# A reordered opening in a fused attention and feed-forward kernel: first values loaded before the last two head pairs, single transposes, four gate steps ahead of the first Silu

## The chip, the cores and the metric

The kernel runs on one core of one Trainium2 chip. The metric is the device time of one execution in microseconds (us), lower is better. Each kernel was run several times. The kernel before took 344.77 us as the median of three runs when the prediction was made.

## The reference

Inputs are `q`, `k`, `v` of shape 8 x 8 x 576 x 64 (batch, heads, sequence, head size) and three weight matrices. It is causal attention with a window of 64, and then a SwiGLU feed-forward over the 4608 tokens.

```python
def _attn_ref(q, k, v):
    scores = scale * np.matmul(q, k.transpose(0, 1, 3, 2))   # scale = 1/8
    rel = pos[:, None] - pos[None, :]
    scores = np.where((rel >= 0) & (rel < 64), scores, -1000000000.0)
    attn = np.exp(scores - np.max(scores, axis=-1, keepdims=True))
    attn = attn / (np.sum(attn, axis=-1, keepdims=True) + 1e-09)
    return np.matmul(attn, v)

def _moe_ref(x, w_gate, w_val, w_out):          # x: 4608 x 512, the heads side by side
    g = x @ w_gate                              # 512 x 1536
    silu = g * (1.0 / (1.0 + np.exp(-g)))
    return silu * (x @ w_val) @ w_out           # 1536 x 512
```

## The kernel before

The 4608 tokens are nine tasks of 512. One task needs scores, exps, sums and values for four pairs of heads, then twelve "gate steps" (each makes one 128-row block of the hidden layer: four matmuls with gate weights, four with value weights), then four projections with their output stores.

Tasks 0 and 1 are the opening. The sync queue loads their q and k as float32, a compute engine casts them to bf16, and the TensorE transposes them. All later tasks are loaded by the GpSimd queue, which casts on the way, and are turned by the VectorE. The first task's values are loaded as float32, cast by GpSimd and copied ("shifted") by the VectorE. Load order and GpSimd's order in the opening:

```python
    for u in range(4):
        load_pair(0, u)                    # q and k of one head pair, 256 KB each
    load_pair(1, 0)
    load_pair(1, 1)
    load_v(nc.sync, staged[0, "v"], 0, (0, 1))
    load_pair(1, 2)
    load_v(nc.sync, staged[0, "v"], 0, (2, 3))
    load_pair(1, 3)
    # ... later, GpSimd (and some VectorE, ScalarE) casts, in this order:
    for u in range(4):
        cast_pair(0, u)
    cast_pair(1, 0)
    cast_pair(1, 1)
    cast_v(0, (0, 1))
    cast_pair(1, 2)
    weights_gv(0, 128)                     # first block of gate and value weights
    cast_v(0, (2, 3))
    cast_pair(1, 3)
    weights_gv(128, 384)                   # second block
    weights_gv(384, 768)                   # third block
    weights_gv(768, 1152)
    load_v(nc.gpsimd, v1[1], 1)
    weights_gv(1152, 1536)
```

GpSimd both casts and issues the weight loads, in program order, so a late cast delays all the weights behind it. The TensorE's side of the opening, with `warm` matmuls that only keep it busy:

```python
    turn_pe(0)
    for i in range(1, 6):
        turn_pe(i)                         # transposes of q and k of pair i
        score(i - 1)
        if i > 2 and i % 2:
            sum_pair(i - 3)
        if i > 3:
            keep_warm(2)
    # ... score(5), turn_pe(6), score(6), sum_pair(4), turn_pe(7), score(7), keep_warm between
    for u in range(4):
        values_of(0, u)
    begun.append(gate_value(0, 0))         # three gate steps before the first Silu
    sum_pair(6)
    begun.append(gate_value(0, 1))
    begun.append(gate_value(0, 2, ps_a.tile([P, 2, 512], FP32, name="gv_ps", tag="a")))
    load_qk(2)                             # GpSimd: q, then k of task 2
    for c in range(2):
        weights_o(6 * c, 6 * c + 6)
    set_silu()                             # the ScalarE's table load: from Exp to Silu
    for m in range(12):
        (begun[m] if m < 3 else gate_value(0, m))()
        # ... task 1's values between them
    for m in range(12):
        gate_value(1, m)()
        if m % 3 == 1:
            turn(2, m // 3)                # VectorE: needs task 2's q and k
```

A gate step ends with a Silu on the ScalarE and a product on the VectorE. A projection's result goes through one of two SBUF buffers to the store:

```python
        def finish():
            nc.scalar.activation(sg[:], g_ps, AF.Silu)
            nc.vector.tensor_mul(hT[t][:, m, :], sg[:], v_ps)
    # in project():
        os_ = fsb.tile([P, 512], FP32, name="os_", tag="os_", bufs=2)
        nc.vector.tensor_copy(os_[:], o_ps[:])
        # ... store os_ with one or four DMAs
```

The softmax here doesn't subtract the row's maximum and nothing guards it: scores larger than these inputs give would overflow.

## Time and profile before

| | before |
|---|---|
| time, median of the runs of this comparison | 344.95 us (four runs, 344.46 to 345.17) |
| span of the profiled run | 342.5 us |
| TensorE busy | 326.3 us, 95% |
| first gate matmul | 25.92 us |
| wait of the fourth gate step | 0.54 us, for the first Silu |
| first transpose of task 2's k | 55.41 us, no wait |
| wait for an output buffer | 1.33 us on the TensorE at 134.51 us |

The page of the kernel before: the span, the busy time of each engine, busy tenths in 40 slices (8.6 us each), and, from the groups of instructions, the gate matmuls with their idle time ahead of them and what ended most of it.

```profile
span 342.5 us, 7084 instructions
PE 326.3 (95%) x2779; PEld 155.6 (45%) x2824; DVE 209.4 (61%) x309; ACT 162.2 (47%) x226; POOL 142.7 (42%) x253
...
PE   7869999999999998999999999999999999999994
...
PEclk9999999999999999999999999999999999999998
...
L286 PE MATMUL g_ps<-xT,wg 128*128 128x512 bf16 x416 | 108.6, 379 | 2.5 <-DVE os__1921 L306 1.3
```

PE is the TensorE. It is idle for 16 us of 342, and the first slices hold most of that.

The timeline of the kernel before (start, duration, engine, line, operation; in brackets the idle time before it and what ended it). SP is the sync engine, POOL is GpSimd, DVE the VectorE, ACT the ScalarE. Here and below single lines are picked from a view; what stands between them is left out.

```profile
17.27 0.90 POOL L157 DMA_DIRECT2D wg<-in_moe_w_gate_dram  x1
20.58 0.69 POOL L393 CAST qk_b<-k_f 128x512 bf16<-128x512 f32 x1
21.22 0.74 POOL L157 DMA_DIRECT2D wg<-in_moe_w_gate_dram  x1
25.92 1.07 PE L286 MATMUL g_ps<-xT,wg 128*128 128x512 bf16 x3 [0.16 <-issue]
32.51 1.02 PE L286 MATMUL g_ps<-xT,wg 128*128 128x512 bf16 x4 [0.54 <-ACT sg L293]
...
34.23 1.03 PE L286 MATMUL g_ps<-xT,wg 128*128 128x512 bf16 x4
...
55.41 1.28 DVE L197 STREAM_TRANSPOSE kT<-k_s 128x512 bf16<-128x512 bf16 x1
58.23 1.03 PE L286 MATMUL v_ps<-xT,wv 128*128 128x512 bf16 x4
...
133.77 0.69 DVE L306 COPY os__1921<-o_ps 128x512 f32<-128x512 f32 x1 [2.56 <-DMA out_dram<-os__1786]
134.51 1.02 PE L286 MATMUL g_ps<-xT,wg 128*128 128x512 bf16 x4 [1.33 <-DVE os__1921 L306]
```

The second weight block is issued at 21.22, straight after the last pair's cast, so the opening's weights hang on those casts. The k transpose at 55.41 starts without a wait, but task 2's k lands, by the packet records, at 55.22: 0.19 us of room.

### The profile page before, as it was taken

The page shows a single profiled execution, that of the slowest core. Times are in us where ns is not written, and L with a number is a line of the kernel's source. Part 1 is how long each engine was busy: PE and PEld are TensorE (multiplying, and loading weights), DVE is VectorE, ACT ScalarE, POOL GpSimd, SP SyncE. Part 2 cuts the span into 40 slices and gives each one's busy share as a digit, 9 for nine tenths or more (in the row PEclk, how much of TensorE's full clock was granted, in tenths as well). Part 3 has the DMA queues.
Part 4 walks back from the last instruction along what each step waited for, and adds up shares of the span by engine and source line. Part 5 has one row for each costly group of instructions (what it writes and reads, how often), then busy time and mean ns, then how long its engine had stood idle before and what let it go on. Part 6 is the DMA issues. An engine that isn't in the chain of part 4 may idle for free.

```text
span 342.5 us, 7084 instructions
## 1 busy us (share of the span) xinstructions
PE 326.3 (95%) x2779; PEld 155.6 (45%) x2824; DVE 209.4 (61%) x309; ACT 162.2 (47%) x226; POOL 142.7 (42%) x253
## 2 busy tenths in 40 slices
PE   7869999999999998999999999999999999999994
PEld 4533444444444453444444544454445444454441
DVE  5663657764456773786478657775777476754431
ACT  3866223353343565347633763376337733673310
POOL 4796469234456995426520989066200000000000
PEclk9999999999999999999999999999999999999998
DMA  7999999998899939919970799879500330020013
GB/s 260 298 140 190 185 166 134 169 227 147 203 202 239 118 61 213 233 30 169 182 178 1 116 184 175 54 123 214 138 2 24 78 78 0 14 82 31 1 34 93
DMA packets 83362, 44.43 MB, mean 130 GB/s; under 512 B 64640, under 2 KB 77952, under 8 KB 83328
## 3 DMA queue, kind: packets, MB, share of 16 engines
q0 software_dynamic: 46656, 21.28, 51.2%
q1 hardware_dynamic: 35744, 21.64, 22.6%
q10 hardware_dynamic: 928, 1.05, 1.1%
q8 instruction: 22, 0.36, 0.4%
q14 instruction: 12, 0.10, 0.1%
HBM read 53.02 MB, written 9.44 MB: 182 GB/s over the span
## 4 chain that ended last, share of the span: by engine, by line
PE 86%; DMA 6%; DVE 2%; POOL 2%; issue 1%; ACT 1%; SPq 1%; DVEq 0%
PE v_ps L286 26%; PE o_ps L301 26%; PE g_ps L286 26%; PE s_ps L219 3%; PE ao_ps L264 2%; PE d_ps L248 2%; DMA v_f<-in_v_dram 2%; DMA out_dram<-os__1786 2%; DMA k_f<-in_k_dram 2%; POOL qk_b L393 1%; DVE xT L270 1%; SPq L318 1%; POOL v L146 1%; SPq L73 0%; ACT L324 0%
## 5 line engine op out<-in xcount | busy, mean ns | idle before, releaser
L293 ACT ACTIVATE sg<-g_ps 128x512 f32<-128x512 f32 x107 | 63.8, 597 | 118.3 <-PE g_ps L286 84.9
L294 DVE TENSOR_TENSOR hT<-sg,v_ps 128x512 bf16<-128x512 f32 x107 | 74.1, 693 | 65.3 <-PE v_ps L286 58.2
L286 PE MATMUL g_ps<-xT,wg 128*128 128x512 bf16 x416 | 108.6, 379 | 2.5 <-DVE os__1921 L306 1.3
L286 PE MATMUL v_ps<-xT,wv 128*128 128x512 bf16 x420 | 108.9, 379 | 0.5
L301 PE MATMUL o_ps<-wo,hT 128*128 128x512 bf16 x407 | 96.8, 380 | 1.4 <-issue 0.3
L107 POOL DMA_DIRECT2D k_s<-in_k_dram x112 | 60.7, 551 | 31.7 <-DMA q_s<-in_q_dram 21.1
L286 PEld LDWEIGHTS <-wg 128*128 128x128 bf16 x432 | 41.8, 98 | 52.4 <-issue 2.8
L286 PEld LDWEIGHTS <-wv 128*128 128x128 bf16 x432 | 42.2, 98 | 51.3 <-issue 0.4
L301 PEld LDWEIGHTS <-hT 128*128 128x128 bf16 x432 | 39.7, 98 | 45.1
L234 ACT ACTIVATE E<-s_ps 128x1024 bf16<-128x1024 f32 x36 | 35.4, 1020 | 14.5 <-PE s_ps L219 9.5
L270 DVE TENSOR_TENSOR xT<-ao_ps,r 128x512 bf16<-128x512 f32 x36 | 24.7, 690 | 19.3 <-ACT r L254 18.1
L197 DVE STREAM_TRANSPOSE kT<-k_s 128x512 bf16<-128x512 bf16 x28 | 35.9, 1283 | 0.0
L253 ACT ACTIVATE r<-d_ps 128x512 f32<-128x512 f32 (+1 forms) x32 | 20.6, 643 | 27.6 <-PE d_ps L248 27.6
L146 POOL CAST v<-v_f 128x512 bf16<-128x512 f32 x24 | 15.4, 652 | 31.4 <-DMA v_f<-in_v_dram 30.1
L236 DVE TENSOR_TENSOR E<-E,mask 128x1024 bf16<-128x1024 bf16 x24 | 17.2, 718 | 10.4 <-ACT E L234 10.3
L87 POOL DMA_DIRECT2D q_s<-in_q_dram x24 | 13.1, 553 | 23.4 <-DVE qT L190 13.8
L254 ACT ACTIVATE r<-r 128x512 f32<-128x512 f32 (+1 forms) x32 | 21.8, 683 | 1.0
L190 DVE STREAM_TRANSPOSE qT<-q_s 128x512 bf16<-128x512 bf16 x28 | 19.7, 704 | 0.0
L264 PEld LDWEIGHTS <-v 128*64 128x64 bf16 x576 | 13.6, 112 | 6.3 <-issue 2.5
L264 PE MATMUL ao_ps<-E,v 128*64 128x64 bf16 x576 | 15.1, 196 | 1.2 <-DVE xT L270 0.8
L248 PE MATMUL d_ps<-E,ones 128*64 128x512 bf16 x72 | 13.6, 393 | 0.9 <-ACT E L234 0.7
L219 PE MATMUL s_ps<-qT,kT 64*64 64x128 bf16 (+1 forms) x640 | 12.9, 211 | 0.8 <-DVE kT L180 0.8
(89 smaller groups left out, 177.5 us busy)
## 6 DMA issues: line engine op xcount, KB each, us to landing
k_s<-in_k_dram POOLq DMA_DIRECT2D x112, 56.0 KB, 4.6
v_f<-in_v_dram SPq DMA_DIRECT2D x24, 256.0 KB
q_s<-in_q_dram POOLq DMA_DIRECT2D x24, 248.0 KB, 6.7
q_f<-in_q_dram SPq DMA_DIRECT2D x8, 256.0 KB
v<-in_v_dram POOLq DMA_DIRECT2D x16, 128.0 KB, 7.7
k_f<-in_k_dram SPq DMA_DIRECT2D x6, 256.0 KB
wo<-in_moe_w_out_dram POOLq DMA_DIRECT2D x2, 768.0 KB, 10.0
v<-v SPq DMA_DIRECT2D x6, 256.0 KB
```

The lines of the kernel that those rows point to most:

```text
L107: nc.gpsimd.dma_start(k_s[p0:p0 + 32, g, :, 0:w], k[b, a:H:2, s:s + P].rearrange("u (r e) d -> r u (e d)", e=4) [:, :, 32 * c:32 * c + w],)
L197: nc.vector.transpose(dst[:, u, :].rearrange("r (g x e) -> r g e x", g=4, e=4), k_s[:, :, u].rearrange("r g (e d) -> r g e d", d=D)[:, :, ...
L219: nc.tensor.matmul(blocks(s_ps[64 * c:64 * c + 64, h], t, lo, hi), zero[r] if src is None else src[r, u, x:x + 64], blocks(qT[r], t, lo, h ...
L234: nc.scalar.activation(E[:], s_ps[:], AF.Exp, scale=0.125)
L253: nc.scalar.activation(x, d_ps[:], AF.Ln)
L254: nc.scalar.activation(x, x, AF.Exp, scale=-1.0)
L264: nc.tensor.matmul(blocks(o_ps[64 * h:64 * h + 64], t, m, m + 1), (v1, v2)[m // 4][t % 2][:, m % 4, 2 * u + h, :] if t == LAST else (v2, v ...
L270: nc.vector.tensor_mul(xT[t][:, u, :], o_ps[:], inverse.pop((t, u)))
L286: nc.tensor.matmul(ps, w[:, c, P * m:P * m + P], xT[t][:, c, :], start=(c == 0), stop=(c == 3),)
L293: nc.scalar.activation(sg[:], g_ps, AF.Silu)
L294: nc.vector.tensor_mul(hT[t][:, m, :], sg[:], v_ps)
L301: nc.tensor.matmul(o_ps[:], hT[t][:, c, P * s:P * s + P], wo[:, c, :], start=(c == 0), stop=(c == 11),)
```

## The change

It should bring the TensorE to its gate steps earlier. The first task's values are loaded and used ahead of the last two head pairs of task 1; q and k get transposes and PSUM buffers of their own; loads and casts are single and stand where they are used; sums stand where their exps end; four gate steps, not three, precede the first Silu, so that the ScalarE's table load is hidden behind more matmuls. The last two weight blocks are also cut into three, task 1's values are loaded after column 1024 of the weights and not after 1152, and the opening has ten warm matmuls, not eight. The diff, cut to its core:

```diff
-    def transposes(t, u):
-        tp = ps_f.tile([P, 2, 512], BF16, name="tp", tag="g")
+    def transposes(t, u, i):
+        tp = ps_f.tile([P, 512], BF16, name="tp", tag="gv"[i])
 # ... one of q and k per call, each copied by the VectorE as before
-    for u in range(4):
-        load_pair(0, u)
-    load_pair(1, 0)
-    load_pair(1, 1)
-    load_v(nc.sync, staged[0, "v"], 0, (0, 1))
-    load_pair(1, 2)
-    load_v(nc.sync, staged[0, "v"], 0, (2, 3))
-    load_pair(1, 3)
+    for i in range(6):
+        load_heads(i // 4, i % 4)
+    load_v(nc.sync, staged[0, "v"], 0)
+    load_heads(1, 2)
+    load_heads(1, 3)
 # ... the block of casts and weights_gv (above) goes; in its place:
+    cast_heads(0, 0, nc.scalar.copy, on_v)
     turn_pe(0)
     for i in range(1, 6):
+        cast_heads(i // 4, i % 4, nc.scalar.copy if i == 1 else on_p, on_p)
         turn_pe(i)
 # ...
-        if i > 3:
+        if i > 2:
             keep_warm(2)
-    shift_v(0, nc.vector.tensor_copy, 0, 2)
     score(5)
     keep_warm(2)
+    for i in range(0, 4, 2):
+        cast_v(0, (i, i + 1))
+        shift_v(0, on_v, i, i + 2)
+    keep_warm(2)
+    weights_gv(0, 128)
+    values_of(0, 0)
+    values_of(0, 1)
+    cast_heads(1, 2, on_p, on_p)
     turn_pe(6)
+    sum_pair(4)
+    values_of(0, 2)
     score(6)
-    sum_pair(4)
-    keep_warm(2)
-    shift_v(0, nc.vector.tensor_copy, 2, 4)
+    cast_heads(1, 3, on_p, on_p)
     turn_pe(7)
+    values_of(0, 3)
+    weights_gv(128, 384)
+    weights_gv(384, 768)
+    weights_gv(768, 1024)
+    load_v(nc.gpsimd, v1[1], 1)
+    weights_gv(1024, 1280)
+    weights_gv(1280, 1536)
     score(7)
-    for u in range(4):
-        values_of(0, u)
     begun.append(gate_value(0, 0))
 # ...
+    begun.append(gate_value(0, 3, wide()))
 # ...
-        (begun[m] if m < 3 else gate_value(0, m))()
+        (begun[m] if m < 4 else gate_value(0, m))()
```

More of the change, by code (lines that the diff above doesn't have):

```diff
@@ L165, in weights_o @@
         )
-    def transposes(t, u):
-        tp = ps_f.tile([P, 2, 512], BF16, name="tp", tag="g")
-        if u == 0:
-            queries[t] = att.tile([P, 4, 512], BF16, name="qT", tag="qT")
-        for i in range(2):
-            for e in range(4):
-                for h in range(2):
-                    nc.tensor.transpose(
-                        tp[64 * h:64 * h + 64, i, P * e:P * e + P],
-                        staged[t][:, i, 2 * u + h, e, :], identb[:],
-                    )
-        nc.vector.tensor_copy(queries[t][:, u, :], tp[:, 0, :])
-        nc.vector.tensor_copy(
-            kT[t % 2][:, u, :].rearrange("p (r e) -> p r e", e=4),
-            tp[:, 1, :].rearrange("p (e r) -> p r e", e=4),
-        )
+    def transposes(t, u, i):
+        tp = ps_f.tile([P, 512], BF16, name="tp", tag="gv"[i])
+        for e in range(4):
+            for h in range(2):
+                nc.tensor.transpose(
+                    tp[64 * h:64 * h + 64, P * e:P * e + P],
+                    staged[t][:, i, 2 * u + h, e, :], identb[:],
+                )
+        if i == 0:
+            nc.vector.tensor_copy(queries[t][:, u, :], tp[:])
+        else:
+            nc.vector.tensor_copy(
+                kT[t % 2][:, u, :].rearrange("p (r e) -> p r e", e=4),
+                tp[:].rearrange("p (e r) -> p r e", e=4),
+            )
     def turn(t, u):
@@ L330, with load_heads @@
     new_v(0)
-    def load_pair(t, u):
+    def load_heads(t, u):
         hs = slice(2 * u, 2 * u + 2)
@@ L385, with cast_heads @@
         staged[t] = cast.tile([P, 2, H, 4, D], BF16, name="qk_b", tag=f"c{t}")
-    def cast_pair(t, u):
+        queries[t] = att.tile([P, 4, 512], BF16, name="qT", tag="qT")
+    def cast_heads(t, u, *copies):
         hs = slice(2 * u, 2 * u + 2)
-        for i in range(2):
-            copy = nc.gpsimd.tensor_copy
-            if t == 0 and u < 2 - i:
-                copy = nc.vector.tensor_copy if i else nc.scalar.copy
+        for i, copy in enumerate(copies):
             copy(staged[t][:, i, hs], raw[t][i][:, hs])
-    for u in range(4):
-        cast_pair(0, u)
-    cast_pair(1, 0)
-    cast_pair(1, 1)
-    cast_v(0, (0, 1))
-    cast_pair(1, 2)
-    weights_gv(0, 128)
-    cast_v(0, (2, 3))
-    cast_pair(1, 3)
-    weights_gv(128, 384)
-    weights_gv(384, 768)
-    weights_gv(768, 1152)
-    load_v(nc.gpsimd, v1[1], 1)
-    weights_gv(1152, 1536)
+    on_v, on_p = nc.vector.tensor_copy, nc.gpsimd.tensor_copy
     def values_of(t, u):
@@ L419, in score, with turn_pe @@
         scores(i // 4, i % 4)
-    def turn_pe(i):
-        transposes(i // 4, i % 4)
+    def turn_pe(i, *which):
+        for x in which or range(2):
+            transposes(i // 4, i % 4, x)
     def sum_pair(i):
@@ L426, in sum_pair, with wide @@
         sums(t, (u, u + 1), ps_a.tile([P, 2, 512], FP32, name="d_ps", tag="a"))
+    def wide():
+        return ps_a.tile([P, 2, 512], FP32, name="gv_ps", tag="a")
+    cast_heads(0, 0, nc.scalar.copy, on_v)
     turn_pe(0)
     for i in range(1, 6):
+        cast_heads(i // 4, i % 4, nc.scalar.copy if i == 1 else on_p, on_p)
         turn_pe(i)
@@ L433 @@
             sum_pair(i - 3)
-        if i > 3:
+        if i > 2:
             keep_warm(2)
-    shift_v(0, nc.vector.tensor_copy, 0, 2)
     score(5)
     keep_warm(2)
+    for i in range(0, 4, 2):
[6 more added lines that the diff above has]
+    cast_heads(1, 2, on_p, on_p)
     turn_pe(6)
+    sum_pair(4)
+    values_of(0, 2)
     score(6)
-    sum_pair(4)
-    keep_warm(2)
-    shift_v(0, nc.vector.tensor_copy, 2, 4)
+    cast_heads(1, 3, on_p, on_p)
     turn_pe(7)
+    values_of(0, 3)
[5 more added lines that the diff above has]
+    weights_gv(1280, 1536)
     score(7)
-    for u in range(4):
-        values_of(0, u)
     begun.append(gate_value(0, 0))
@@ L450 @@
     begun.append(gate_value(0, 1))
-    begun.append(gate_value(0, 2, ps_a.tile([P, 2, 512], FP32, name="gv_ps", tag="a")))
+    begun.append(gate_value(0, 2, wide()))
+    begun.append(gate_value(0, 3, wide()))
     load_qk(2)
```

## The prediction

> **What bounds it now.** The TensorE is 95% busy (busy shares); from 32.5 us on the timeline shows gate, value and projection matmuls almost back to back (one gate step: 1.73 us). Only the opening has holes: the first gate matmul starts at 25.92, and the fourth gate step at 32.51, after a 0.54 us wait for the first Silu.
>
> Behind the opening stands the DMA. By the packet records, the last sync-queue loads (task 1, pair 3) land at 19.8 and about 20.3, and GpSimd casts them at 20.02 and 20.58 (timeline). The first gate/value weights are issued at 17.27, the second block at 21.22, right after those casts. From about 24 us the GpSimd queue streams without a break: second block landed 25.2/27.0, third 29.5/31.4, fourth 33.4/35.3, task 1's values 36.2 to 38.7, last weights 40.6/42.6, task 2's q 43.8 to 47.8, its k 48.2 to 55.22. The VectorE's first transpose of that k starts at 55.41: only 0.2 us of room.
>
> **What the change does.** The value products (four of 0.37 us, serialised by 0.69 us evictions from 23.42 to 25.9) move ahead of and between the last two head pairs, transposes get a buffer per half, one sums group moves forward, and four gate steps instead of three precede the first Silu.
>
> The Trainium skill ("DMA: Bandwidth & Descriptors", Queues, rings and completion order) says that each DMA engine round-robins between queues and consumes each ring in order (the loads' semaphores here do complete in issue order); putting values ahead of pairs moves no total: the last pair should still land near 20. GpSimd does four value casts (0.61 each), two weight issues (0.8 each), four pair casts: the second weight block is issued at 21.2 to 21.7, no earlier than now; the weight stream is 0 to 0.3 late.
>
> **Estimate.** The last q/k casts end near 21.4, and then the VectorE does copies (0.42, 0.68) and evictions (0.69) in order: first gate matmul near 24.5 to 25. The sums' Ln and Exp, table load and Silu follow; the fourth step no longer waits for the Silu but for its value weights (31.4 to 31.7). The fifth step, 34.23 now, starts near 32.4: TensorE about 1.8 us ahead. The first turn then wants k at 53.6, but it lands at 55.2 to 55.5. The VectorE works in order, so the next hT product ends no earlier than now (57.2), and the value matmul of task 1's step 4 (58.23 now) gains only 1.0 less the stream's lateness. Gain 0.8 us.
>
> **Predicted time 344.0 us, 342.7 to 344.9 (8 in 10).** Faster by over 2%: 0.01; within 2%: 0.98; slower: 0.01.
>
> **What would show it.** First gate matmul at 24 to 25.3. Second weight block issued at 21 to 21.8 and landed at 25 to 27.5. Fourth gate step waiting for weights, not for the Silu. In the waits, a new one of the VectorE's k transpose for the k DMA, 1 to 2 us, near 54, and a TensorE hole of 0.5 to 1.2 us near 57. After 60 us the same schedule, shifted by under 1.2 us.
>
> **What would make it wrong.** If the earlier values let GpSimd issue the second weight block clearly before 20.5, the stream and task 2's k move up and up to 2 us are gained. If port conflicts between VectorE copies and GpSimd slow the casts ("SBUF — State Buffer", Who interferes with whom; here a cast took 0.90 instead of 0.61 us at 15.68 beside a VectorE copy), the stream is later and the gain vanishes.

## The result, and the profile after

The kernel after took 343.58 us as the median of four runs (342.99 to 343.94) beside 344.95 us before. The ratio is 0.996, with a 95% interval of 0.994 to 0.998, so it is the same by the 2% rule. Here and below a ratio is the mean time of one kernel's runs over that of the other's runs of the same rounds, so not quite the ratio of the medians.

The page of the kernel after, the same parts, and from the groups the k transposes:

```profile
span 342.2 us, 7134 instructions
PE 329.9 (96%) x2826; PEld 156.2 (46%) x2826; DVE 209.1 (61%) x309; ACT 162.2 (47%) x226; POOL 143.6 (42%) x255
...
PE   7969999999999999999999999999999999999994
...
PEclk9989999999999999999999999999999999999999
...
L196 DVE STREAM_TRANSPOSE kT<-k_s 128x512 bf16<-128x512 bf16 x28 | 36.0, 1284 | 1.6 <-DMA k_s<-in_k_dram 1.6
```

Two things are new: the third slice has a lower clock, and the k transposes, which waited for nothing before, wait 1.6 us for the k DMA. The TensorE's busy time is 3.6 us higher in a span 0.3 us shorter. That is hardly more work done (two more warm matmuls): part of it is matmuls at half clock, and some matmul records can be missing from a trace (before lists 2779 matmuls beside 2824 weight loads, after 2826 beside 2826).

The timeline of the kernel after, for the same places:

```profile
19.50 0.61 POOL L388 CAST qk_b<-q_f 128x512 bf16<-128x512 f32 x1 [0.89 <-DMA q_f<-in_q_dram]
20.17 0.41 PE L172 MATMUL tp<-identb,qk_b 128*64 128x128 bf16 x8 [2.00 <-POOL qk_b L388]
22.00 0.74 POOL L157 DMA_DIRECT2D wg<-in_moe_w_gate_dram  x1
25.53 1.04 PE L285 MATMUL g_ps<-xT,wg 128*128 128x512 bf16 x4
...
32.85 1.04 PE L285 MATMUL gv_ps<-xT,wv 128*128 128x512 bf16 x4 [0.45 <-DMA wv<-in_moe_w_val_dram]
33.73 1.03 PE L285 MATMUL g_ps<-xT,wg 128*128 128x512 bf16 x4
...
56.60 1.32 DVE L196 STREAM_TRANSPOSE kT<-k_s 128x512 bf16<-128x512 bf16 x1 [1.62 <-DMA k_s<-in_k_dram]
58.49 1.02 PE L285 MATMUL v_ps<-xT,wv 128*128 128x512 bf16 x4 [0.61 <-DVE hT L293]
...
133.44 0.69 DVE L305 COPY os__1932<-o_ps 128x512 f32<-128x512 f32 x1 [1.96 <-DMA out_dram<-os__1797]
134.18 1.02 PE L285 MATMUL g_ps<-xT,wg 128*128 128x512 bf16 x4 [0.73 <-DVE os__1932 L305]
```

Line by line against before: the first gate matmul is only 0.39 us earlier (25.92 to 25.53). The fifth step is 0.50 us earlier (34.23 to 33.73). The first k transpose is 1.19 us **later** (55.41 to 56.60), because k lands later (56.32 by the packet records, 55.22 before). The matmul behind it is 0.26 us later (58.23 to 58.49). So at 58 us the changed kernel is behind. At 134 us it is ahead again by 0.33 us, since the wait for the output buffer is 0.73 and not 1.33 us. That 0.33 us then stays to the end (spans 342.5 and 342.2).

### The half-clock stretch

The windows view gives busy times in stretches that I cut at the clock's own steps, which come every 3.41 us (3413 ns). Columns: stretch, its length, busy time (and instructions) of PE, PEld, DVE, ACT and POOL, granted clock, mean busy share of the DMA engines, GB/s. The kernel before:

```profile
15.99:19.40 3.41, 2.32 (x62) 1.34 (x50) 1.87 (x4) 2.59 (x3) 3.41 (x5) 1.00 0.85 223
19.40:22.81 3.41, 2.17 (x28) 0.97 (x24) 2.96 (x4) 2.99 (x3) 3.41 (x7) 1.00 0.81 78
```

The kernel after:

```profile
18.31:21.72 3.41, 1.32 (x36) 0.96 (x36) 1.90 (x4) 0.08 (x2) 2.42 (x5) 1.00 0.95 136
21.72:25.13 3.41, 3.24 (x80) 2.49 (x78) 2.37 (x5) 2.97 (x3) 3.41 (x6) 0.50 0.55 68
```

Before, the TensorE is 2.32 and 2.17 us busy in the two stretches (68% and 63%), and the clock stays at 1.00. After, the 2.00 us wait ahead of the transposes at 20.17 leaves only 1.32 us busy (39%), and the next stretch runs at 0.50. The Trainium skill ("TensorE: Matmul & The Clock Gate", What's actually happening) says that the clock is judged in a free-running window of 3413 ns and has two states, half and full; the step lengths here agree. It names as the rule "no PE-idle gaps >~3.4µs" (HAM oscillation); here a hole of 2.00 us was enough. The same load was late in most traces of the changed opening (see e1), and what the half clock cost is sorted out under e9 to e11.

### The profile page after: what moved, and what is told of

It reads as the page before. It is cut to its first block, busy times and chain, and to the rows that moved or that the text cites. A ratio compares the mean times of both kernels' runs of the same rounds, so it can differ in the third digit from the quotient of the medians.

```text
span 342.2 us, 7134 instructions
## 1 busy us (share of the span) xinstructions
PE 329.9 (96%) x2826; PEld 156.2 (46%) x2826; DVE 209.1 (61%) x309; ACT 162.2 (47%) x226; POOL 143.6 (42%) x255
## 4 chain that ended last, share of the span: by engine, by line
PE 83%; DMA 8%; SPq 3%; DVE 1%; POOL 1%; ACT 1%; issue 1%; DVEq 0%
PE g_ps L285 26%; PE v_ps L285 26%; PE o_ps L300 25%; DMA wv<-in_moe_w_val_dram 3%; PE ao_ps L263 2%; PE s_ps L218 2%; PE d_ps L247 2%; DMA out_dram<-os__1797 2%; DMA q_f<-in_q_dram 2%; SPq L126 2%; DMA k_f<-in_k_dram 1%; SPq L317 1%; POOL qk_b L388 1%; ACT E L233 1%; DMA out_dram<-os__1734 0%
## 5 line engine op out<-in xcount | busy, mean ns | idle before, releaser
L300 PE MATMUL o_ps<-wo,hT 128*128 128x512 bf16 x432 | 99.0, 380 | 0.0
L263 PEld LDWEIGHTS <-v 128*64 128x64 bf16 x576 | 14.4, 113 | 5.9 <-DVE v L153 1.4
L263 PE MATMUL ao_ps<-E,v 128*64 128x64 bf16 x576 | 16.0, 197 | 0.8 <-DVE v L153 0.8
```

The source lines that it names most:

```text
L263: nc.tensor.matmul(blocks(o_ps[64 * h:64 * h + 64], t, m, m + 1), (v1, v2)[m // 4][t % 2][:, m % 4, 2 * u + h, :] if t == LAST else (v2, v ...
L300: nc.tensor.matmul(o_ps[:], hT[t][:, c, P * s:P * s + P], wo[:, c, :], start=(c == 0), stop=(c == 11),)
```

## The experiments

The question was why so little arrives, and whether the gain lies where the traces put it. The expectations name two theories, and those of the later groups say for themselves what they expect. Theory A says that the traces tell the whole story: the opening gains some time, and what it gains is taken or given where the schedule meets a DMA, at k (55 us) and at the output store (133 us). The rival, theory B, says that most of the measured 1.4 us is a gain that comes through to the end whatever happens at these two places. All twelve runs gave correct results, with five rounds each. One yardstick for all of them: how many microseconds a trace is ahead of the first trace of the kernel before, by the end times of the VectorE's products and copies (positive is ahead).

| kernel | at 51 us (last product of task 0) | 84 us (after the k transposes) | 155 us (after the stores) | last copy |
|---|---|---|---|---|
| after | +0.50 | −0.26 | +0.34 | +0.33 |
| e1 after, again | +2.01 | +0.80 | +1.61 | +1.59 |
| e2 before, four output buffers | +0.04 | +0.04 | +1.53 | +1.53 |
| e3 after, four output buffers | +0.85 | +0.04 | +1.54 | +1.52 |
| e4 after, later turns | +0.88 | +0.88 | +2.37 | +2.37 |
| e5 before, both | −0.09 | −0.09 | +1.39 | +1.39 |
| e6 after, both | +0.27 | +0.27 | +1.76 | +1.76 |
| e7 = e5 with four gate steps | +0.98 | +0.98 | +2.47 | +2.47 |
| e8 = e6, last pair cast on VectorE | +0.65 | +0.65 | +2.14 | +2.14 |
| e9 = e6 with six warm matmuls | +1.41 | +1.41 | +2.90 | +2.90 |
| e10 = e9, last pair cast on VectorE | +1.49 | +1.49 | +2.98 | +2.98 |
| e11 = e9 with three gate steps | +1.10 | +0.03 | +1.53 | +1.52 |
| e12 = e5 without warm matmuls in the loop | −2.80 | −2.80 | −1.31 | −1.31 |

The times, each beside the kernel before on the same chip. The three groups ran on three different chips, so times are compared within a group. The mean of a "before" row takes in all eleven runs; the ratio leaves out the first of them, which isn't among the timed rounds. Between two experiments of a group, the six runs of each leave a difference of means uncertain by 0.5 to 1.1 us (95%, my estimate from their scatter). Of the differences below only e6 against e5, e10 against e9 and, just, e4 against e1 are clear of zero.

| run | median us (lowest to highest) | mean us | ratio to before (95%) |
|---|---|---|---|
| before, group 1 | 343.91 (342.78 to 347.49) | 344.34 | |
| e1 | 343.86 (342.12 to 345.00) | 343.64 | 0.9989 (0.9958 to 1.0019) |
| e2 | 343.07 (342.66 to 343.72) | 343.14 | 0.9975 (0.9949 to 1.0001) |
| e3 | 342.69 (342.46 to 343.21) | 342.76 | 0.9963 (0.9941 to 0.9986) |
| e4 | 342.21 (341.84 to 343.16) | 342.38 | 0.9952 (0.9928 to 0.9977) |
| before, group 2 | 344.75 (343.24 to 348.30) | 345.27 | |
| e5 | 343.26 (342.59 to 343.68) | 343.21 | 0.9938 (0.9889 to 0.9988) |
| e6 | 341.86 (341.26 to 342.83) | 341.98 | 0.9900 (0.9845 to 0.9955) |
| e7 | 343.27 (341.76 to 343.74) | 342.94 | 0.9930 (0.9879 to 0.9982) |
| e8 | 341.54 (340.63 to 342.72) | 341.57 | 0.9891 (0.9840 to 0.9942) |
| before, group 3 | 344.17 (342.78 to 346.56) | 344.33 | |
| e9 | 342.55 (341.32 to 343.50) | 342.49 | 0.9947 (0.9913 to 0.9980) |
| e10 | 341.16 (340.88 to 341.90) | 341.27 | 0.9911 (0.9880 to 0.9942) |
| e11 | 342.18 (341.42 to 343.62) | 342.30 | 0.9941 (0.9907 to 0.9975) |
| e12 | 344.39 (344.06 to 345.88) | 344.74 | 1.0006 (0.9970 to 1.0041) |

### e1: the kernel after, unchanged, once more

The edit is none.

> The changed kernel unchanged, as the base for the others and to see how much its holes vary. Expected 343.5 us, 0.4% under the kernel before. Profile: VectorE's first k transpose waits for its k DMA 1 to 2 us near 55, PE hole of 0.4 to 0.9 us near 58, PE near 60 us no more than 0.5 us ahead of the kernel before; the wait for the output store at 133 us (1.33 us of PE before, 0.73 in the first profile of the changed kernel) 0 to 1 us.

Measured: 343.86 us, a ratio of 0.9989 to before, with an interval that holds 1. The 1.37 us of the first comparison didn't repeat. The trace of e1, timeline and then windows:

```profile
23.77 1.04 PE L285 MATMUL g_ps<-xT,wg 128*128 128x512 bf16 x4
...
31.36 1.04 PE L285 MATMUL gv_ps<-xT,wv 128*128 128x512 bf16 x4 [0.72 <-DMA wv<-in_moe_w_val_dram]
...
55.54 1.32 DVE L196 STREAM_TRANSPOSE kT<-k_s 128x512 bf16<-128x512 bf16 x1 [2.06 <-DMA k_s<-in_k_dram]
...
132.92 1.02 PE L285 MATMUL g_ps<-xT,wg 128*128 128x512 bf16 x4 [0.53 <-DVE os__1932 L305]
```

```profile
17.65:21.06 3.41, 2.08 (x62) 1.55 (x62) 2.40 (x4) 0.93 (x2) 3.41 (x7) 1.00 1.22 228
21.06:24.48 3.42, 2.99 (x80) 1.87 (x79) 2.31 (x5) 3.32 (x4) 3.42 (x5) 1.00 0.74 83
```

The same instructions, in another run: the TensorE is 61% busy in the first window, the next one keeps the full clock, and the first gate matmul starts at 23.77 and not 25.53. In this run k lands at 55.27, so the k transpose waits longer (2.06 us) than in the first trace and starts sooner, and 1.2 of the 2.0 us lead are lost there. The opening therefore has two outcomes from run to run. In the first trace the load of q of pair (1,2) landed late: by the packet records 15 of its 16 DMA engines were done at 17.78 and the last at 19.45. In e1 the last was done at 18.37, 0.25 us behind the others. The late outcome is the usual one: in the other eight traces of the changed opening (after, e3, e4, e6, e8 to e11) the last engine was 0.81 to 1.73 us behind.

### e2 and e3: four output buffers in the kernel before, and in the kernel after

```diff
-        r = fsb.tile([P, 2, 512], FP32, name="r", tag="r", bufs=4)
+        r = fsb.tile([P, 2, 512], FP32, name="r", tag="r", bufs=3)
-        os_ = fsb.tile([P, 512], FP32, name="os_", tag="os_", bufs=2)
+        os_ = fsb.tile([P, 512], FP32, name="os_", tag="os_", bufs=4)
```

The room for the two buffers comes from `r`, since the SBUF is full.

> Kernel before with four output buffers instead of two (paid for by three instead of four buffers for the inverse sums). The PE wait of 1.33 us at 133 us on the output store of two tiles earlier goes. Theory A (the whole gain of the change comes from a shorter store wait at 133 us, since by 60 us its lead is gone): 1.3 us faster than the kernel before, 343.6, as fast as the changed kernel. Theory B (the opening itself gains about 1.3 us that lasts): also 1.3 faster here, but then the changed kernel with four buffers is faster by another 1.3. Opening identical to the kernel before.

> Changed kernel with four output buffers. Theory A: 0.7 us faster than the changed kernel at most, and 0 to 0.3 us SLOWER than the kernel before with four buffers (the PE stood 0.26 us behind the kernel before at 60 us in the first profiles). Theory B: 1.3 us faster than the kernel before with four buffers, near 342.3.

Measured: 343.07 and 342.69 us. In the trace of e2 the wait at the store is gone. Its timeline there:

```profile
132.12 1.03 PE L286 MATMUL v_ps<-xT,wv 128*128 128x512 bf16 x4
132.98 1.03 PE L286 MATMUL g_ps<-xT,wg 128*128 128x512 bf16 x4
```

This matmul stood at 134.51 with 1.33 us of idle time before it. Now it stands at 132.98 with none, and the gain of 1.49 us (+0.04 to +1.53 in the table) stays to the end of this trace. The times show less: a ratio of 0.9975, about 0.9 us, with an interval that just holds 1. In e3 the k transpose is late as in the first trace of after:

```profile
56.30 1.32 DVE L196 STREAM_TRANSPOSE kT<-k_s 128x512 bf16<-128x512 bf16 x1 [1.65 <-DMA k_s<-in_k_dram]
```

So in e3 0.81 of the 0.85 us lead are lost at k, and e2 and e3 end level in their traces (+1.53, +1.52). The means differ by 0.38 us in favour of the changed opening, which is within their scatter (0.47 us). Theory A had 0 to 0.3 us slower, theory B 1.3 us faster: the traces fit A, the times speak against B and don't tell 0.38 from none. e3 also had a half-clock window, after one with 28% TensorE busy time.

### e4: later turns in the kernel after

```diff
         gate_value(1, m)()
-        if m % 3 == 1:
+        if m % 3 == 2:
             turn(2, m // 3)
```

Each turn of task 2 comes one gate step (1.73 us) later, so k may land later.

> Changed kernel, task 1's four turns of task 2's q and k one gate step (1.73 us) later, so that the first k transpose does not wait for its DMA. Both theories: k wait under 0.3 us, no PE hole at 58 us, PE 0.4 to 0.6 us ahead of the kernel before at 60 us. Theory A: the store wait at 133 us takes it back (its landing is set by the DMA load, not by the PE), so the time is that of the changed kernel within 0.3. Theory B: 0.7 us faster than the changed kernel.

Measured: 342.21 us, 1.25 us under e1 by the means (ratio 0.9963). The timeline of e4:

```profile
56.85 1.32 DVE L196 STREAM_TRANSPOSE kT<-k_s 128x512 bf16<-128x512 bf16 x1 [0.52 <-DMA k_s<-in_k_dram]
...
132.14 1.03 PE L285 MATMUL g_ps<-xT,wg 128*128 128x512 bf16 x4
```

The k transpose still waits 0.52 us, but no TensorE hole follows, and the lead of 0.88 us passes 84 us whole. What I had expected of the store was wrong: I thought that the two output buffers would take the lead back. Instead the wait vanished, and the lead grew by 1.49 us, as with four buffers. The landings of the four output stores show how. Before, stores 2 to 4 landed at 129.99, 131.35 and 133.65, among the GpSimd queue's q loads (issued 125.57 to 127.17). In e4 those loads were issued at nearly the same times (125.51 to 127.12), but the four stores 0.87 us earlier (123.83 to 126.01 in place of 124.71 to 126.88). They landed at 126.23, 127.23, 127.42 and 129.80. So the store's wait depends, as far as these landings show, on how far the stores come ahead of the other stream, and here 0.9 us of lead was enough. That is how the gain of an early stage can grow on its way.

### e5 to e8: a harness without the two traps

Both edits together (four output buffers and later turns) were put in the kernel before (e5) and in the kernel after (e6). Neither of these has a wait at the store or a hole behind k, so the opening is compared by itself. e7 is e5 with only the fourth gate step, and e8 is e6 with one GpSimd burden moved.

```diff
 # e7, against e5
+    begun.append(gate_value(0, 3, ps_a.tile([P, 2, 512], FP32, name="gv_ps", tag="a")))
-        (begun[m] if m < 3 else gate_value(0, m))()
+        (begun[m] if m < 4 else gate_value(0, m))()
 # e8, against e6
-    cast_heads(1, 3, on_p, on_p)
+    cast_heads(1, 3, on_v, on_v)
```

> Kernel before in a harness that takes both later traps away: four output buffers (no store wait at 133 us) and task 1's four turns one gate step later (room for task 2's k). Its end then shows what the opening is worth. Expected as the kernel before with four output buffers, 343.1 on the last chip (0.9975 of the kernel before), since the kernel before did not wait for k: within 0.3 us of it.

> Changed kernel in the same harness. Theory A (the opening is worth what the hT products showed before 55 us, a lead of 0.5 to 2.0 us, and the plain kernel loses most of it at k): 0.5 to 1.2 us faster than the kernel before in the harness. Theory B (the opening is worth nothing, the change lives on the store wait): equal within 0.3 us. Lead over the kernel before's first trace at hT product 12 near 0.9 and kept to the store; no k wait, no store wait.

> Kernel before in the harness plus the fourth gate step ahead of the first Silu alone (none of the reordering). In the kernel before the fourth step waited from 31.59 to 32.51 for the Silu; its weights had landed at 29.5 and 31.4. If the fourth step is the part that pays, it is 0.8 to 0.9 us faster than the kernel before in the harness, as much as the whole change; if the reordering of values and pairs pays, within 0.3 us of the kernel before in the harness.

> Changed kernel in the harness with the last pair's two casts on the VectorE (0.43 us each) instead of GpSimd (0.61 us each), so that GpSimd issues the second weight block 1.2 us earlier. If GpSimd's casts hold the weight stream: second block issued near 20 to 20.8 instead of 21 to 22, fourth block's landing 1 us earlier, no wait of the fourth step for its weights, and 0.4 to 0.8 us faster than the changed kernel in the harness. If the DMA engines themselves hold it: stream and time as they were.

Measured: e5 took 343.21 us by the mean, the microseconds that I had expected, but the kernel before was slower on this chip (345.27), so the ratio is 0.9938 and not 0.9975. e6 over e5 is 0.9964, 1.22 us by the means, give or take 0.6, and at the upper end of this group's theory A. So with the traps gone the changed opening is worth about 1.2 us. The profiled run of e6 shows less, 0.37 us (+1.76 and +1.39), for its weights were late. It also holds a half-clock window (after one 51% busy). The timeline of e6 at the fourth gate step:

```profile
33.09 1.04 PE L285 MATMUL gv_ps<-xT,wv 128*128 128x512 bf16 x4 [0.85 <-DMA wv<-in_moe_w_val_dram]
```

Of e6's six runs, the two with a mean granted clock of 0.993 and 0.995 took 342.47 and 342.83 us; the four of 0.997 to 1.0 took 341.26 to 341.92. All runs are sorted by their clock below.

e7 gave a trace lead of 1.08 us over e5 (+2.47 and +1.39) and 0.27 us by the means. The profiled run of e7 had the full clock, but four of its six runs had not (mean clock 0.992 to 0.995, 343.16 to 343.74 us); the two that had took 342.08 and 341.76. So the 1.08 us show in the times only when runs of like clock are compared (below), which leaves two runs of e7 and four of e5.

e8 was 0.42 us under e6 by the means (0.9988), within the scatter. GpSimd issued the second weight block at 20.64 instead of 21.67 us, and the fourth gate step no longer waited for weights. So GpSimd's cast load does set when the weights come. What that is worth isn't settled here: this trace had a half-clock window and its first gate matmul only at 26.00. The same edit in e10, at full clock, is worth 1.22 us.

### e9 to e11: filling the hole

```diff
 # e9, against e6
     values_of(0, 1)
+    hold = ps_a.tile([P, 2, 512], FP32, name="hold", tag="a")
+    for _ in range(6):
+        nc.tensor.matmul(hold[0:D, 0], ones[:, 0:D], ones[:])
     cast_heads(1, 2, on_p, on_p)
 # e10, against e9
-    cast_heads(1, 3, on_p, on_p)
+    cast_heads(1, 3, on_v, on_v)
 # e11, against e9: three gate steps ahead of the Silu, not four
-    begun.append(gate_value(0, 3, wide()))
-        (begun[m] if m < 4 else gate_value(0, m))()
+        (begun[m] if m < 3 else gate_value(0, m))()
```

> Changed kernel in the harness, with six warm matmuls (0.22 us each) in the TensorE hole near 18 to 20 us, where the changed opening waits for the casts of the last two pairs. Theory C: that hole leaves the 3.41 us clock window it falls in under about 0.55 busy (0.28 to 0.51 in five of six traces of the changed opening, 0.61 and more in every window that kept its clock), and the next window runs at half clock, which costs the opening 1 us. Then: no half-clock window in the opening, first gate matmul 23.7 to 24.8 instead of 25.4, time 0.6 to 1.2 us under the changed kernel in the harness (341.98 mean on the last chip). Rival: the half clock costs nothing, because the weights' landing binds: first gate earlier, but the fourth step waits longer, and the time is that of the changed kernel in the harness within 0.3.

> The same warm matmuls plus the last pair's casts on the VectorE, the candidate for the best version. Expected: no half-clock window, second weight block issued near 20.3, 0.3 to 0.6 us under the warm harness kernel, so 340.6 to 341.2, and about 1% under the kernel before.

> The warm harness kernel with three instead of four gate steps ahead of the first Silu. In the kernel before's order the fourth step was worth 1.1 us in the trace. If it is the fourth step that pays in the changed kernel too, 0.6 to 1.0 us slower than the warm harness kernel. If with the reordering the fourth step waits for its value weights (about 31.3) anyway, within 0.3 us of it.

Measured: e9's timeline, and its window with the warm matmuls:

```profile
24.06 0.81 PE L285 MATMUL g_ps<-xT,wg 128*128 128x512 bf16 x3 [0.16 <-issue]
31.95 1.04 PE L285 MATMUL gv_ps<-xT,wv 128*128 128x512 bf16 x4 [0.52 <-DMA wv<-in_moe_w_val_dram]
```

```profile
15.64:19.05 3.41, 3.27 (x64) 1.94 (x64) 2.86 (x5) 2.88 (x3) 3.08 (x5) 1.00 1.00 296
```

The window is 96% busy, the clock stays full, and the first gate matmul starts at 24.06, near e1's 23.77. All six runs of e9 had a mean clock of 0.998 or more. The lead at 51 us is 1.41 us where e6 had 0.27. The times didn't follow: e9's ratio to before is 0.9947, e6's was 0.9900 on another chip. I had expected 0.6 to 1.2 us under e6; it isn't shown.

The lead of the trace isn't the clock's either. Here are the traces of the changed opening with GpSimd's casts and four early steps. "Last k landed" is the k of pair (1,3), by the packet records; the value weights are those of the fourth gate step.

| trace | clock in the opening | last k landed | first gate matmul | value weights landed | value matmuls of the fourth step start |
|---|---|---|---|---|---|
| e1 | full | 20.31 | 23.77 | 31.31 | 31.36 |
| e9 | full | 20.57 | 24.06 | 31.90 | 31.95 |
| e6 | half in one window | 21.05 | 25.36 | 33.04 | 33.09 |
| e4 | half in one window | 21.29 | 25.54 | 32.43 | 32.47 |
| e3 | half in one window | 21.34 | 25.74 | 32.47 | 32.51 |
| after | half in one window | 21.39 | 25.53 | 32.81 | 32.85 |

From the last k to the first gate matmul it took 3.46 and 3.49 us at full clock, and 4.14 to 4.40 with a half-clock window. So a late load costs the first gate matmul its own lateness, and the half clock 0.7 to 0.9 us on top. But in all six the fourth step's value matmuls start 0.04 or 0.05 us after their weights have landed, whatever the clock was. The landing binds there, and the lead at 51 us follows it: e9 is 1.14 us ahead of e6 in both. This is the rival named in the expectation of e9, and on what binds these traces side with it; its forecast of an equal time is untested, since e6 and e9 ran on different chips. In these six traces the half clock cost no time that the wait for the weights would not have taken; where the weights come early (e8, e10) or the half clock lasts (e12) it may.

What the warm matmuls do show is the steady clock: all eighteen runs of e9, e10 and e11 were at 0.997 or above, while only seven of the twelve of e6 and e8 were.

e10 was 1.22 us under e9 by the means (0.9964, give or take 0.8 us), with 341.16 us as its median. That is the best of group 3. Its second weight block was issued at 20.55 where e9's was at 21.18, and its fourth step has no wait, though its first gate matmul is late, as the timeline of e10 shows:

```profile
25.39 0.81 PE L285 MATMUL g_ps<-xT,wg 128*128 128x512 bf16 x3 [0.16 <-issue]
...
31.88 1.03 PE L285 MATMUL gv_ps<-xT,wv 128*128 128x512 bf16 x4
```

e10 beats both kernels: its ratio to before is 0.9911 (0.988 to 0.9942), and its slowest run (341.90) is faster than the fastest of before (342.78). Against the kernel after there is no run on the same chip; the ratios to before, 0.9911 and 0.996 or 0.9989, put it 0.5 to 0.8% ahead.

e11 took 0.19 us less than e9 by the means, with a scatter of 1.0 us, so no worth of the fourth gate step is shown in the changed opening. In the traces e11 is 0.31 us behind e9 at 51 us. Its timeline shows why so little:

```profile
31.41 1.02 PE L285 MATMUL g_ps<-xT,wg 128*128 128x512 bf16 x4 [0.45 <-ACT sg L292]
```

With three steps ahead the fourth waits 0.45 us for the first Silu; with four it waits 0.52 us for its value weights (e9). One wait nearly replaced the other. e11 fell into the k trap again all the same (+1.10 to +0.03): later turns leave room, but not always enough.

### e12: the kernel before (e5), without the warm matmuls of its loop

```diff
         if i > 2 and i % 2:
             sum_pair(i - 3)
-        if i > 3:
-            keep_warm(2)
 # ... and the keep_warm(2) after score(5) and after sum_pair(4)
```

> Kernel before in the harness without its eight warm matmuls inside the opening loop. If a window under about 0.55 busy halves the next one's clock, the windows near 16 to 23 (0.61 to 0.74 busy with them) fall to about 0.5, a half-clock window appears in the opening, and it is 0.4 to 1.2 us slower than the kernel before in the harness (343.2 mean). If only a wholly idle window halves the clock, no half-clock window and the same time within 0.3.

Measured: 344.39 us, a ratio of 1.0006 to before, where e5 had 0.9938 on another chip. The windows of e12:

```profile
13.68:17.09 3.41, 1.67 (x34) 0.83 (x33) 1.45 (x3) 3.38 (x4) 2.23 (x4) 1.00 0.93 230
17.09:20.50 3.41, 2.48 (x34) 1.22 (x34) 2.13 (x4) 1.77 (x3) 3.41 (x7) 0.50 1.05 201
...
23.92:27.33 3.41, 2.65 (x69) 2.27 (x67) 2.28 (x4) 1.02 (x1) 3.41 (x5) 0.50 1.32 158
27.33:30.74 3.41, 3.41 (x11) 0.94 (x9) 0.30 (x1) 0.00 (x0) 2.07 (x4) 0.50 1.28 194
```

One window 49% busy brings the half clock, and three windows of 73 to 78% busy don't end it; only after one that is 100% busy is the full clock back. The lead at 51 us is −2.80, 2.71 us behind e5. The first gate matmul is at 27.17 (25.79 in e5), and the value weights of the fourth step wait for the TensorE (landed 31.67, used from 36.08), so here the clock does bind. An opening at half clock for 13.65 us can thus cost 2.7 us, and what kept e5 from it were these eight warm matmuls, as far as two traces show (all six runs of e12 had a mean clock below 0.997, two of six of e5). The longest single hole doesn't tell the windows apart: it was 1.15 us at the window that halved the clock in e12, and 1.20 us in e1, where the clock stayed full. Over all traces, between 5 us and the first Silu:

| busy share of a window at full clock | the next window's clock |
|---|---|
| 0.28 (e3), 0.39 (after), 0.39 (e8), 0.44 (e4), 0.49 (e12), 0.51 (e6) | half |
| 0.61 (e1), 0.61 (e5), 0.61 (e10), 0.62 (e2), 0.62 (e7), 0.63 (before), and all above | full |

### All runs sorted by their clock

After the experiments I sorted every run of the three groups by its mean granted clock over the execution. One stretch of 3.41 us at half clock lowers that mean by 3.41 x 0.5 / 342 = 0.005, so 0.997 and above stands for a run without one in the opening. (After its last matmul a run ends at half clock too; in the traces that takes up to 2.26 us, or 0.003.) Only for the profiled runs is it known where the low clock lay. Mean us (number of runs):

| kernel | clock 0.997 and above | below 0.997 |
|---|---|---|
| before, group 1 | 343.56 (6) | 345.27 (5) |
| e1 | 343.18 (2) | 343.87 (4) |
| e2 | 342.89 (4) | 343.64 (2) |
| e3 | 342.84 (2) | 342.72 (4) |
| e4 | 342.53 (3) | 342.24 (3) |
| before, group 2 | 343.73 (3) | 345.85 (8) |
| e5 | 343.05 (4) | 343.52 (2) |
| e6 | 341.65 (4) | 342.65 (2) |
| e7 | 341.92 (2) | 343.45 (4) |
| e8 | 340.93 (3) | 342.20 (3) |
| before, group 3 | 343.95 (6) | 344.78 (5) |
| e9 | 342.49 (6) | none |
| e10 | 341.27 (6) | none |
| e11 | 342.30 (6) | none |
| e12 | none | 344.74 (6) |

Three things follow. First, in nine of the eleven rows that have both kinds, the runs of lower clock are longer, by 0.5 to 2.1 us; e3 and e4 are the exceptions. A line through all 105 runs, each against the mean of its kernel and group, gives 0.93 us for 0.005 of clock (correlation −0.64). This is an association: a late load can bring the hole, the lower clock and late weights all at once, as the table under e9 shows. Second, more than half of the runs of the kernel before (18 of 33) were of the lower kind, though its one profile of the first comparison was not. That goes with much of its scatter, and may be part of why one trace and a median disagree. Third, runs of like clock agree with some of the traces and not with others: at full clock e7 is 1.13 us under e5 (trace 1.08), and e10 is 2.68 us under before (trace 2.98), but e2 is 0.67 under before (trace 1.53), e5 0.68 (trace 1.39) and e9 1.46 (trace 2.90). One trace is one run. e8 is 2.80 us under its before at full clock, so what e10 has over it is mainly that it stays there. By the same reading e9 is 1.46 us under before and e6 2.08, so the warm matmuls may cost something where the clock would have been full anyway; two chips and six runs don't settle that.

## Why the prediction was right or wrong

The predicted 344.0 us (342.7 to 344.9) held: 343.58 us, 0.4% under before. The steps:

- **The DMA stands behind the opening: right.** The fourth gate step waits for its value weights and no longer for the Silu (0.45 us at 32.85), as foretold. That the fourth step is then worth little fits e11, whose time doesn't differ from e9's by more than the scatter.
- **"the second weight block is issued at 21.2 to 21.7": mis-sized.** It was issued at 22.00 and landed by 27.86, not by 27.5. The cause is the late q load: its cast waited 0.89 us (19.50), and GpSimd's later work moved with it. In e1, where that load came in time, the block was issued at 20.92. The last pair, which "should still land near 20", landed at 20.72 and 21.39 (19.64 and 20.31 in e1; 19.82 and 20.50 in before, where the prediction has 20.3). I argued from totals ("moves no total") and didn't ask what happens if one load of the sync queue lands late.
- **"first gate matmul near 24.5 to 25": mis-sized.** It was 25.53. The step left out is that the TensorE, having done the values early, has nothing to do until the pair (1,2) comes: a 2.00 us hole, and then a window at half clock. The kernel before had put warm matmuls where it waited. By the table under e9 about 0.7 us of this is the half clock's, and the rest is the late load's (last k at 21.39). e9 filled the hole: full clock, and the first gate matmul at 24.06. e1, without the half clock, had 23.77.
- **"the TensorE about 1.8 us ahead" at the fifth step: mis-sized.** It was 0.50 us ahead (33.73). The term that failed is the landing of the fourth step's value weights: 32.81, not 31.4 to 31.7. The TensorE can't be further ahead than that, and the fifth step follows 0.92 us later. In e1 they landed at 31.31, and the fifth step stood at 32.23, 2.0 us ahead. So the form of the estimate was right, and the lateness of the weights (the second block and those behind it) is what it missed.
- **"the first turn then wants k ... The VectorE works in order": right.** The k transpose waited 1.62 us (1 to 2 predicted), and the TensorE hole was 0.61 us (0.5 to 1.2 predicted). e4 moved the turns, and the loss was gone.
- **"gains only 1.0 less the stream's lateness": right as a form, mis-sized in its term.** The lateness of task 2's k was 1.10 us (56.32 against 55.22), not 0 to 0.3. The formula gives −0.10 and the matmul was −0.26: the gain of 0.8 us was not there at 58 us.
- **"After 60 us the same schedule": wrong.** At the output store the wait fell from 1.33 to 0.73 us, which gave 0.59 us back. I had called the TensorE "almost back to back" from 32.5 us on and passed over the 1.3 us that the page of before showed for `os__1921`. In the trace of e2 this wait alone is worth 1.49 us, more than the whole predicted gain (about 0.9 us by the times).
- **The two risks that I named: neither came.** The second block was never issued before 20.5 us in the kernel after (22.00, and 20.92 in e1), and the cast that was late (19.50) took 0.61 us, so a port conflict didn't slow it: it started late. What the Trainium skill says of each ring being consumed in order ("DMA: Bandwidth & Descriptors", Queues, rings and completion order) agrees: the sync queue's loads completed in issue order in both traces.

The number was right partly by luck, because two misses cancel: the opening gave less than predicted, and the store gave something that wasn't predicted. How much of the measured 1.37 us is the change's own isn't settled. The first pair of traces has 0.33 us, the repetition (e1; the chip of the first comparison isn't on record) 0.05 us by the medians and 0.1% by the ratio, which is 0.4 us. With both traps out of the way it is 1.22 us (e6 against e5), or 1.40 us when only the runs at full clock are taken. Of its parts only the fourth gate step was tried alone (e7, e11); values first, single transposes and the moved sums were not. Why the last load lags isn't settled either. In before, of the values' second load 15 engines were done at 13.46 and the 16th at 14.98; there a 16 KB packet of instruction fetch of 0.94 us starts at 12.39. In after, such packets start at 11.93 and 16.81 (1.23 us), and q's last engine is late at 19.45. The records don't name the engine, so this is a coincidence in time and not a shown cause. It speaks against a simple link that e1 had such a packet of 1.24 us at 16.14 as well, and there q's last engine was only 0.25 us behind. The Trainium skill ("Runtime: NRT & Kernel Launch", Instruction fetch mechanics) tells of refills in 16 KiB blocks whose cost is "mostly hidden"; the packet sizes agree, and no run here tests the cost.

## What to carry to other kernels

Before an early stage is credited with a gain, follow the lead through the trace to every later place where compute meets a DMA (a load with little room, a buffer that waits for its store): each may swallow the lead, and some give more than the lead itself (here 1.49 us in the trace for two more output buffers). When work is pulled ahead of a load, look at the hole that it leaves: on this core a 3.4 us window that was at most half busy cost half the clock in the next, and six matmuls without use kept it. Then ask what binds behind the hole: a full clock brought the first gate matmul forward, but the fourth step still began when its weights had landed. For changes of under 1%, repeat the comparison and look at runs of like clock: the unchanged kernel after gave 0.996 and 0.9989, and its opening had two different outcomes.

## What the Trainium skill lacked or had wrong

- "TensorE: Matmul & The Clock Gate" (HAM oscillation, Part 1) gives the rule of no idle gaps over about 3.4 us. Here shorter holes were enough, and the busy share of one 3.41 us window sorts the cases: windows with 0.28 to 0.51 busy (after: a 2.00 us wait, 1.32 of 3.41 us busy) were followed by half clock, all those with 0.61 or more kept it. The page also tells of a kernel whose frequent short idle stretches made the clock swing, but it gives no such share.
- The same page (What's actually happening) says that one busy, sustained window brings full clock back, and not how busy it must be. In e12 windows 0.73, 0.75 and 0.78 busy didn't; one that was 1.00 busy did. In after a window 0.95 busy did (3.24 of 3.41 us), in e8 one of 0.90.
- "DMA: Bandwidth & Descriptors" (Latency and other measured facts) says that two of the 16 DMA engines are usually slower and guesses at the GpSimd queue's descriptors. Here one engine of 16 lagged by 1.5 us (13.46 and 14.98) on a sync-queue load, before the first GpSimd load was issued (17.27), and by 0.92 to 1.52 us on that load in all fourteen traces. The records don't say whether it is one of those two, and the cause is open.
- "Runtime: NRT & Kernel Launch" (Instruction fetch mechanics) gives no duration for a fetched block. Here the 22 packets of 16 KB in before took 0.88 to 1.73 us on the DMA (median 0.97).
